# Beacon keys and first weights of a fused attention and MLP kernel: smaller loads, other queues, values split by even and odd d

## The chip, the cores and the metric

One core of a Trainium2 chip. The metric is the device time of one execution in microseconds (us), lower is better. All runs quoted are in the fast state unless said; the runs of one kernel spread over 0.1% to 1.4%. All kernels gave the reference's result.

## The reference

Attention over 8 batches of 8 heads, 576 queries and keys of width 64. Sixteen unmasked "beacon" keys and values stand ahead of the causal ones. The result, 4608 tokens of 512, goes through a two-layer MLP with a hidden width of 2048.

```python
k_all = np.concatenate([beacon_k, k], axis=2)          # 16 + 576 keys
v_all = np.concatenate([beacon_v, v], axis=2)
scores = scale * np.matmul(q, k_all.transpose(0, 1, 3, 2))
scores = np.where(causal, -1e9, scores)                # beacons are never masked
a = softmax(scores)
x = np.matmul(a, v_all)  ->  (B*S, H*D) = (4608, 512)
h = x @ w_in                                           # 512 x 2048
out = (h * sigmoid(1.702 * h)) @ w_out                 # 2048 x 512
```

## The kernel before

The heads are worked on in 16 sets of four, two sets to a batch; "set 2" is the first set of the second batch. The program first makes a list of operations with estimated durations and dependencies, runs a small scheduler over it, and issues every engine's instructions in the order that it found. Each engine then works through its own queue strictly in that order: **an instruction that waits holds up everything behind it on its engine**, whatever the scheduler had assumed of the wait. The traces show it: in the kernel before a cast waits 7.11 us on VectorE and the normalisation behind it starts at 26.98; with the cast moved (experiment 9) it starts at 19.86. That is what this case turns on.

The beacon keys of all sets stand in one tile, `bkf`, 32 partitions to a head. Loads of 32 rows fill the 32 partitions, though a head has 16 beacon rows; the other 16 are another head's. Sets 0 and 1 are loaded first; the rest is loaded in one batch after the first exponential:

```python
def e_load_bk(a, s0, s1):                      # head a of four, sets s0 to s1
    for u, e, nr in (...):                     # nr = 32 rows, 16 at the very end
        nc.sync.dma_start(
            out=bkf[32 * a : 32 * a + nr, u:e, :],
            in_=bass.AP(..., ap=[[D, nr], [Q * Nb * D, e - u], [1, D]]))
...
load_bk(0, HS)                                 # HS = 2: sets 0 and 1
...
            if (s, c) == (0, 0):
                later = op("DVE", 60, [exps[(0, 0)]], lambda: nc.vector.memset(bkf[:, HS, 0:1], 0.0), name="bk")
                load_bk(HS, NSET, [later])     # sets 2 to 15 at once
```

A set's keys begin with a cast of its beacon rows on VectorE; the transposes of keys and queries follow. "due" is a time before which the scheduler doesn't place an operation:

```python
cast = op(
    "DVE", 80, [ld_bk[s]] + turn.get((s - 2, 1), []), lambda: e_bk(s),
    pr=0 if urgent else 4, due=max(0, due_of(s, 0) - 10000), name=f"bk{s}",
)
```

The first weights, w1, are loaded by GpSimd in 16 transfers of 128 KB (as kept), four for each quarter of the columns. The rows are picked so that a chunk of 128 fits a half of each head's width: heads `a`, half `x`, row `r`:

```python
def e_load_w1(kt, c0, c1):
    hs, x = divmod(kt, 2)
    nc.gpsimd.dma_start(
        out=w1t[:, kt, c0:c1],
        in_=moe_w_in[:, c0:c1].rearrange("(g a x r) n -> g x a r n", g=HS, a=Q, x=2)[hs, x])
...
lhs = vb[b % NB2][0:kw, j, Q * hs + h, HD * x : HD * x + HD]     # values, half x of d
```

## Time and profile before

| before | value |
|---|---|
| time, median of 3 runs | 357.74 us (357.34 to 358.22) |
| span of the profiled execution | 355.7 us |
| TensorE busy, idle | 330.5 us, 25.2 us |
| beacon loads after the first exponential | three of 112 KB, one of 104 KB, one of 4 KB, on SP |
| their landing | 7.0 to 10.1 us after issue |
| w1 | 16 transfers, first issue at 7.8, last landing at 32.8 us |

Only TensorE is busy for most of the span (330.5 us; VectorE 202.1, ScalarE 201.3, GpSimd 113.2), so a microsecond of its idle time is a microsecond of the kernel. Some 20 of its 25 us of idle time lie in the first 27.5 us (13.1 and 7.3 in two stretches), so the start is what to read. The prediction below shows the lines.

The pages of DMA packets of the kernel before are needed later (queue, packets, MB, and the time that its packets took as a share of 16 engines' span; q0 is GpSimd's):

```profile
DMA packets 61223, 29.04 MB, mean 82 GB/s; under 512 B 48384, under 2 KB 52480, under 8 KB 61184
...
q0 software_dynamic: 53824, 18.51, 46.9%
```

### The profile page before, as it was taken

Reading aid. Unit: us, or ns where it says so; the run is one execution under the profiler, and the core shown is the slowest. Engines: PE = TensorE matmul, PEld = TensorE weight load, DVE = VectorE, ACT = ScalarE, POOL = GpSimd, SP = SyncE. Lnnn points to the kernel's source line nnn. Section 1 sums busy time; section 2 is a strip of 40 time slices with the busy share of each in tenths; the row PEclk is TensorE's granted clock in tenths of the full one; section 3 lists DMA queues with packets and bytes.
Section 4 is the critical chain, followed back from the end, with each engine's and each line's share of the span. In section 5 each row is a group of like instructions: output and inputs, shape, how many; then the busy total and the mean of one; then the engine's idle time right before and its main releaser. Section 6 shows DMA issues by size and latency. Waiting matters only on the chain.

```text
span 355.7 us, 9039 instructions
## 1 busy us (share of the span) xinstructions
PE 330.5 (93%) x3904; PEld 169.8 (48%) x3904; DVE 202.1 (57%) x385; ACT 201.3 (57%) x245; POOL 113.2 (32%) x192
## 2 busy tenths in 40 slices
PE   0529999999999999999999999999999999999995
PEld 0416665555545454545454545545445444444442
DVE  2816786768975759476665748485435444333300
ACT  1425577588856667776666576676553444444421
POOL 8746457257141913271264317230300000000000
PEclk9999999999999999999999999999999999999999
DMA  7999999259232942393439147800000110010011
GB/s 132 145 155 156 209 185 188 68 100 97 41 51 78 81 88 50 79 103 92 100 21 156 38 97 64 120 31 31 31 30 31 41 48 31 29 59 31 29 74 74
DMA packets 61223, 29.04 MB, mean 82 GB/s; under 512 B 48384, under 2 KB 52480, under 8 KB 61184
## 3 DMA queue, kind: packets, MB, share of 16 engines
q0 software_dynamic: 53824, 18.51, 46.9%
q1 hardware_dynamic: 7360, 9.96, 8.0%
q8 instruction: 30, 0.49, 0.6%
q14 instruction: 9, 0.07, 0.1%
HBM read 37.48 MB, written 9.44 MB: 132 GB/s over the span
## 4 chain that ended last, share of the span: by engine, by line
PE 82%; DMA 11%; POOL 3%; issue 1%; ACT 1%; DVE 1%; POOLq 0%; ACTq 0%
PE u L521 34%; PE u L488 32%; PE u L437 9%; PE s L374 7%; DMA w<-in_moe_w_in_dram 5%; DMA w<-in_moe_w_out_dram 4%; DMA qn<-in_q_dram 2%; POOL vb L308 1%; DVE g L509 1%; POOL kn L287 0%; POOL qn L287 0%; POOL E L413 0%; ACT sig L502 0%; ACT osb L535 0%; ACT E L385 0%
## 5 line engine op out<-in xcount | busy, mean ns | idle before, releaser
L509 DVE SCALAR_TENSOR_TENSOR g<-sig,u 128x512 f16<-128x512 f16 x144 | 97.6, 685 | 102.2 <-ACT sig L502 102.1
L488 PE MATMUL u<-xT,w 128*128 128x512 f16 (+1 forms) x640 | 147.5, 361 | 7.6 <-DVE xT L466 7.2
L521 PE MATMUL u<-w,g 128*128 128x512 f16 x576 | 143.8, 379 | 0.0
L502 ACT ACTIVATE sig<-u 128x512 f16<-128x512 f32 x144 | 85.2, 597 | 95.0 <-PE u L488 94.1
L385 ACT ACTIVATE E<-s 128x2048 f16<-128x2048 f32 (+2 forms) x64 | 99.6, 1556 | 35.4 <-PE s L374 34.8
L488 PEld LDWEIGHTS <-w 128*128 128x128 f16 x640 | 59.6, 98 | 69.0 <-DMA w<-in_moe_w_in_dram 7.5
L521 PEld LDWEIGHTS <-g 128*128 128x128 f16 x576 | 54.9, 98 | 65.0 <-issue 0.2
L413 POOL TENSOR_SCALAR_AFFINE_SELECT E<-E 128x448 f16<-128x448 f16 (+2 forms) x84 | 43.1, 538 | 123.5 <-ACT E L385 123.5
L374 PE MATMUL s<-qT,kT 32*128 32x288 f16 (+4 forms) x1152 | 37.0, 251 | 13.3 <-DVE kT L350 10.5
L374 PEld LDWEIGHTS <-kT 32*128 32x128 f16 x1152 | 22.8, 96 | 40.1 <-issue 25.9
L535 ACT ACTIVATE osb<-u 128x512 f32<-128x512 f32 x36 | 21.5, 598 | 20.0 <-PE u L521 19.9
L437 PE MATMUL u<-E,vb 128*32 128x288 f16 (+4 forms) x1024 | 29.9, 257 | 0.0
L308 POOL DMA_DIRECT2D vb<-in_v_dram x32 | 27.2, 871 | 2.7 <-DMA qn<-in_q_dram 1.6
L466 DVE TENSOR_TENSOR xT<-u,rz 128x288 f16<-128x288 f32 x64 | 26.5, 451 | 2.7 <-DVE rz L457 0.5
L437 PEld LDWEIGHTS <-vb 128*32 128x32 f16 (+1 forms) x1024 | 22.3, 98 | 2.8
L448 DVE STREAM_TRANSPOSE zt<-u 128x288 f32<-128x288 f32 x32 | 15.4, 480 | 11.5 <-PE u L437 11.5
L359 DVE STREAM_TRANSPOSE qT<-qn 128x576 f32<-128x576 f32 x16 | 19.9, 1241 | 1.6 <-PE s L374 1.6
L359 DVE STREAM_TRANSPOSE kT<-kn 128x576 f32<-128x576 f32 x16 | 20.1, 1257 | 0.6
L437 PE MATMUL u<-E,ones 128*32 128x288 f16 (+4 forms) x512 | 18.1, 260 | 0.4 <-ACT E L385 0.3
L457 DVE STREAM_TRANSPOSE rz<-rc 128x288 f32<-128x288 f32 x32 | 15.3, 478 | 1.1
L315 POOL DMA_DIRECT2D w<-in_moe_w_in_dram x16 | 10.8, 678 | 7.7 <-DMA w<-in_moe_w_in_dram 5.8
L437 PEld LDWEIGHTS <-ones 128*32 128x32 f16 (+1 forms) x512 | 11.0, 97 | 4.6 <-issue 2.1
(23 smaller groups left out, 52.8 us busy)
## 6 DMA issues: line engine op xcount, KB each, us to landing
out_dram<-osb SPq DMA_DIRECT2D x36, 256.0 KB, 2.0
kn<-in_k_dram POOLq DMA_DIRECT2D x16, 288.0 KB, 5.6
qn<-in_q_dram POOLq DMA_DIRECT2D x16, 288.0 KB, 5.5
vb<-in_v_dram POOLq DMA_DIRECT2D x24, 128.0 KB, 5.4
w<-in_moe_w_in_dram POOLq DMA_DIRECT2D x16, 128.0 KB, 8.4
w<-in_moe_w_out_dram POOLq DMA_DIRECT2D x4, 512.0 KB, 11.4
vb<-in_v_dram POOLq DMA_DIRECT2D x8, 112.0 KB, 3.6
vb<-in_v_dram POOLq DMA_DIRECT2D x8, 80.0 KB, 5.3
```

Source lines behind the costliest of these rows:

```text
L308: nc.gpsimd.dma_start(out=t[0 : hi - lo, j, h0:h1, :], in_=v[b, h0:h1, lo:hi, :].rearrange("h n d -> n h d"),)
L359: nc.vector.transpose(out=f32(dst.rearrange("p n e -> p (n e)")).rearrange("p (r t) -> p t r", t=n), in_=f32(src[:, o : o + n * D]).rearra ...
L374: nc.tensor.matmul(sc[:, h, o : o + e - a], kT[s % NB2][r : r + 32, j * P : (j + 1) * P, d], qT[s % NB2][r : r + 32, a:e, d], start=(d == ...
L385: nc.scalar.activation(out=Es[s][:, :, base[c] : base[c] + w], in_=ss[(s, c)][:, :, 0:w], func=AFT.Exp, scale=0.125,)
L413: nc.gpsimd.affine_select(out=blk, in_=blk, compare_op=ALU.is_ge, fill=0.0, base=off + (Nb if j == 0 else 0), pattern=[[0, Q], [1, w]], ch ...
L437: nc.tensor.matmul(u[32 * h : 32 * h + 32, a - q0 : e - q0], lhs, E[0:kw, h, col : col + e - a], start=(i == 0), stop=(i == n - 1),)
L466: nc.vector.tensor_tensor(out=xT[:, 2 * hs + x, t0 : t0 + HF], in0=rings[("av", s, x, half)][:, 0:HF], in1=zs[(s, half)][1][:, :], op=ALU. ...
L488: nc.tensor.matmul(u[:, o : o + w], w1t[:, kp, nt * P : (nt + 1) * P], xT[:, kp, t0:t1], start=(kp == 0), stop=(kp == NKT - 1),)
L502: nc.scalar.activation(out=sig[:, 0:w], in_=rings[("m1", g, n0)][:, 0:w], func=AFT.Tanh, scale=0.851)
L509: nc.vector.scalar_tensor_tensor(out=gts[g][:, n0:n1, 0:w], in0=sigs[(g, n0)][:, 0 : n * w].rearrange("p (n w) -> p n w", n=n), scalar=1.0 ...
L521: nc.tensor.matmul(o[:, :], gts[g][:, nt, mt * P : (mt + 1) * P], w2t[:, nt, :], start=(nt == 0), stop=(nt == NNT - 1),)
L535: nc.scalar.mul(out=osb[:, :], in_=rings[("m2", g, mt)][:, :], mul=0.5)
```

## The change

The intent: load only the beacon rows that are needed and clear the rest with a memset; put the loads of the very first set on two hardware queues (SP and ACT); load sets 2 and 3 right after the first exponential and the others later; give w1 as eight transfers of plain consecutive rows, which makes the values' halves the even and the odd columns of d; have at most eight of GpSimd's loads in flight in the scheduler's plan; and move the due times of the attention chunks a little. The plan's own reckoning of a beacon load changes with it: before, the data counted as there when the issue ends, now 2.5 us after that. Dead code (filler matmuls, split loads) goes too. Core of the diff:

```diff
-    nc.vector.memset(bkf[P - 32 : P, NSET - 1, :], 0.0)
+    nc.vector.memset(bkf[:, 0:1, :], 0.0)
+    nc.vector.memset(bkf[:, 1:HS, :], 0.0)
...
-    def e_load_w1(kt, c0, c1):
-        hs, x = divmod(kt, 2)
+    def e_load_w1(hs, c0, c1):
         nc.gpsimd.dma_start(
-            out=w1t[:, kt, c0:c1],
-            in_=moe_w_in[:, c0:c1].rearrange("(g a x r) n -> g x a r n", g=HS, a=Q, x=2)[hs, x],
+            out=w1t[:, 2 * hs : 2 * hs + 2, c0:c1],
+            in_=moe_w_in[2 * P * hs : 2 * P * (hs + 1), c0:c1].rearrange("(p x) n -> p x n", x=2),
         )
...
-    def e_load_bk(a, s0, s1):
-        (loads of 32 rows on nc.sync, see above)
+    def e_load_bk(a, s0, s1, e):
+        (nc.sync if e == "SP" else nc.scalar).dma_start(
+            out=bkf[32 * a : 32 * a + Nb, s0:s1, :],
+            in_=beacon_k.rearrange("b (g a) n d -> a n (b g) d", a=Q)[a][:, s0:s1, :],
+        )
...
-                    lhs = vb[b % NB2][0:kw, j, Q * hs + h, HD * x : HD * x + HD]
+                    lhs = vb[b % NB2][0:kw, j, Q * hs + h, x::2]
...
-    T_ATT0, T_ATT1 = 20000, 250000
+    T_ATT0, T_ATT1 = 15000, 255000
...
+    LANES = 8
+    flight = []
     def pool_load(dur, ns, deps, emit, due=0, pr=0, name=""):
+        if len(flight) >= LANES:
+            deps = list(deps) + [flight[-LANES]]
...
-    load_bk(0, HS)
+    load_bk(0, 1, (), ("SP", "ACT"))
+    load_bk(1, HS)
...
-                later = op("DVE", 60, [exps[(0, 0)]], lambda: nc.vector.memset(bkf[:, HS, 0:1], 0.0), name="bk")
-                load_bk(HS, NSET, [later])
+                for s0, s1, due in ((HS, 2 * HS, 12000), (2 * HS, NSET, 60000)):
+                    empty = op(
+                        "DVE", 60 * (s1 - s0), [exps[(0, 0)]],
+                        lambda s0=s0, s1=s1: nc.vector.memset(bkf[:, s0:s1, :], 0.0), due=due, pr=1, name="bk",
+                    )
+                    load_bk(s0, s1, [empty])
```

More of the change, by code (lines that the diff above doesn't have):

```diff
@@ L25, with __init__ @@
     LAT = {"PE": 230, "ACT": 100, "DVE": 135, "POOL": 60, "Q": 1400, "SP": 0}
-    def __init__(self, ring, filler=None, fill_from=1100, fill_to=15500):
-        self.filler, self.fill_from, self.fill_to = filler, fill_from, fill_to
+    def __init__(self, ring):
         self.ops = []
@@ L69, in run @@
         order = []
-        if self.filler:
-            o = self.op("-", 0, [], lambda: None)
-            self.ops.pop()
-            o.start, o.end = 0, self.fill_to
-            self.closers["fill"] = [o]
-            self.bank[-1] = "fill"
-            self.tiles["fill"] = len(self.bank) - 1
-            free["PE"] = self.fill_from
         todo = len(self.ops)
@@ L98, in run @@
             t, e = best
-            if self.filler and e == "PE" and free["PE"] < self.fill_to and t - free["PE"] > 400:
-                n = int((t - free["PE"] - 300) / 216)
-                if n > 0:
-                    o = self.op("PE", 0, [], lambda n=n: self.filler(n), kind="fill")
-                    self.ops.pop()
-                    o.start, o.end = free["PE"], t
-                    order.append(o)
-                    mode = "m"
             ok = []
@@ L135, in run @@
                 lat = self.LAT[o.eng] if u.eng != o.eng or o.eng in ("Q", "DVE", "POOL", "ACT") else 0
-                lat = 1200 if u.eng == "Q" else lat
+                if u.eng == "Q":
+                    lat = 300 if o.eng == "SP" else 1200
+                elif o.name == "bk" and o.eng != "DVE":
+                    lat = 2500
                 u.ready = max(u.ready, o.end + lat)
@@ L279, in ring_tile, with rows_of, e_load_qk @@
         return rings[key]
-    def e_load_qk(s, which, a, e):
+    def rows_of(t, s):
         b, hs = divmod(s, HS)
-        src, dst = ((q, qn), (k, kn))[which]
-        w = (e - a) // 32 * D
-        o = a // 32 * D
-        nc.gpsimd.dma_start(
-            out=dst[s % NB3][:, o : o + w],
-            in_=src[b, Q * hs : Q * hs + Q, a:e, :].rearrange("h (r t) d -> h r (t d)", r=32)
-            if e - a < S
-            else src[b, Q * hs : Q * hs + Q].rearrange("h (r t) d -> (h r) (t d)", r=32),
-        )
+        return t[b, Q * hs : Q * hs + Q].rearrange("h (r t) d -> (h r) (t d)", t=TR)
+    def e_load_qk(s, which):
+        dst = (qn, kn)[which][s % NB3]
+        nc.gpsimd.dma_start(out=dst[:, :], in_=rows_of((q, k)[which], s))
     def e_load_v(b, j, h0, h1):
@@ L325, in e_load_w2 @@
         )
-    def e_load_bk(a, s0, s1):
-        for u, e, nr in ((s0, min(s1, NSET - 1), 32), (max(s0, NSET - 1), s1, Nb)) if a == Q - 1 else (
-            (s0, s1, 32),
-        ):
-            if u < e:
-                nc.sync.dma_start(
-                    out=bkf[32 * a : 32 * a + nr, u:e, :],
-                    in_=bass.AP(
-                        tensor=beacon_k.tensor,
-                        offset=beacon_k.offset + (Q * u + a) * Nb * D,
-                        ap=[[D, nr], [Q * Nb * D, e - u], [1, D]],
-                    ),
-                )
+    def e_load_bk(a, s0, s1, e):
[3 more added lines that the diff above has]
+        )
     def e_bk(s):
@@ L345, in f32, with e_turn @@
         return ap.bitcast(F32)
-    def e_turn(s, which, a, e):
-        if which == 1 and a == 0:
+    def e_turn(s, which):
+        if which == 1:
             nc.vector.transpose(
@@ L353, in e_turn @@
             )
-        dst, src = (qT[s % NB2][:, a:e, :], qn[s % NB3])
+        dst, src = (qT[s % NB2][:, :, :], qn[s % NB3])
         if which == 1:
-            dst, src = (kT[s % NB2][:, Nb + a : Nb + e, :], kn[s % NB3])
-        n = (e - a) // 32
-        o = a // 32 * D
+            dst, src = (kT[s % NB2][:, Nb:NK, :], kn[s % NB3])
         nc.vector.transpose(
-            out=f32(dst.rearrange("p n e -> p (n e)")).rearrange("p (r t) -> p t r", t=n),
-            in_=f32(src[:, o : o + n * D]).rearrange("p (t c) -> p t c", t=n),
+            out=f32(dst.rearrange("p n e -> p (n e)")).rearrange("p (r t) -> p t r", t=TR),
+            in_=f32(src[:, :]).rearrange("p (t c) -> p t c", t=TR),
         )
@@ L548, in due_of @@
         return 0 if s < HS else T_ATT0 + T_CH * (4 * (s - HS) + c)
+    LANES = 8
+    flight = []
     def pool_load(dur, ns, deps, emit, due=0, pr=0, name=""):
+        if len(flight) >= LANES:
+            deps = list(deps) + [flight[-LANES]]
         i = plan.op("POOL", dur, deps, emit, due=due, pr=pr, name=name)
-        return plan.op("Q", ns, [i], lambda: None, name=name + "q")
+        flight.append(plan.op("Q", ns, [i], lambda: None, name=name + "q"))
+        return flight[-1]
     op = plan.op
@@ L559, with load_bk, load_qk @@
     chunks = []
-    SPLIT = 0
-    def parts(s):
-        return [(0, HF), (HF, S)] if s < SPLIT else [(0, S)]
-    def load_bk(s0, s1, deps=()):
-        got = [op("SP", 450, list(deps), lambda a=a: e_load_bk(a, s0, s1), name="bk") for a in range(Q)]
-        for s in range(s0, s1):
-            ld_bk[s] = got[-1]
-    def load_qk(s, which, i, due=0):
-        a, e = parts(s)[i]
-        dep = turn.get((s - NB3, which), [])
-        ld_qk[(s, which, i)] = pool_load(
-            560, 2.7 * (e - a) + (150 if e - a < S else 0), dep, lambda: e_load_qk(s, which, a, e),
-            due=due, name=f"ldqk{s}",
-        )
+    def load_bk(s0, s1, deps=(), queues=("SP",)):
+        got = []
+        for a in range(Q):
+            e = queues[a % len(queues)]
+            got.append(op(e, 450, list(deps), lambda a=a, e=e: e_load_bk(a, s0, s1, e), pr=0, name="bk"))
+        for s in range(s0, s1):
+            ld_bk[s] = got
+    def load_qk(s, which, due=0):
+        dep = [turn.get((s - NB3, which))]
+        ld_qk[(s, which)] = pool_load(560, 1560, dep, lambda: e_load_qk(s, which), due=due, name=f"ldqk{s}")
     def load_v(b, j, due=0):
@@ L588, in load_batch @@
             for which in (1, 0):
-                load_qk(s, which, 0, max(0, due_of(s, 0) - 22000))
+                load_qk(s, which, max(0, due_of(s, 0) - 22000))
         for j in range(-1, NJ):
@@ L594, in load_w1, with turns @@
         return [
-            pool_load(650, 5 * (c1 - c0) // 4 + 120, [], lambda kt=kt: e_load_w1(kt, c0, c1), due=due, name="w1")
-            for kt in range(NKT)
-        ]
-    def turn_part(s, i):
-        a, e = parts(s)[i]
+            pool_load(700, 5 * (c1 - c0) // 2, [], lambda hs=hs: e_load_w1(hs, c0, c1), due=due, name="w1")
+            for hs in range(HS)
+        ]
+    def turns(s):
         urgent = s < HS
-        if i == 0:
-            cast = op(
-                "DVE", 80, [ld_bk[s]] + turn.get((s - 2, 1), []), lambda: e_bk(s),
-                pr=0 if urgent else 4, due=max(0, due_of(s, 0) - 10000), name=f"bk{s}",
-            )
-        for which in (1, 0):
-            deps = [ld_qk[(s, which, i)]]
-            if i == 0:
-                deps += [qks.get((s - NB2, c)) for c in range(4)]
-                deps += [cast] if which else []
-            else:
-                deps += [qks[(s, 0)]]
-            turn.setdefault((s, which), []).append(
-                op(
-                    "DVE", 1.9 * (e - a) + (140 if which and not i else 0), deps,
-                    lambda which=which: e_turn(s, which, a, e),
-                    pr=i if urgent else 4, due=max(0, due_of(s, 0) - 9000), name=f"turn{s}",
-                )
+        cast = op(
+            "DVE", 80, ld_bk[s] + [turn.get((s - 2, 1))], lambda: e_bk(s),
+            pr=0 if urgent else 4, due=max(0, due_of(s, 0) - 10000), name=f"bk{s}",
+        )
+        for which in (1, 0):
+            deps = [ld_qk[(s, which)], cast if which else None]
+            turn[(s, which)] = op(
+                "DVE", 1095 + 140 * which, deps + [qks.get((s - NB2, c)) for c in range(4)],
+                lambda which=which: e_turn(s, which),
+                pr=0 if urgent else 4, due=max(0, due_of(s, 0) - 9000), name=f"turn{s}",
             )
@@ L623, in chunk @@
         if c == 0:
-            turn_part(s, 0)
-        deps = turn[(s, 0)] + turn[(s, 1)] + [exps[chunks[-1]] if chunks else None]
+            turns(s)
+        deps = [turn[(s, 0)], turn[(s, 1)]] + [exps[chunks[-1]] if chunks else None]
         chunks.append((s, c))
@@ L634, in chunk @@
         qks[(s, c)] = pe
-        if c == 0 and len(parts(s)) > 1:
-            turn_part(s, 1)
         exps[(s, c)] = op(
@@ L685, in w2_rows @@
         w2_ld.append(pool_load(750, 2600, [], lambda: e_load_w2(c), name="w2"))
-    load_bk(0, HS)
-    for s in range(HS):
-        load_qk(s, 1, 0)
-        load_qk(s, 0, 0)
-    keeps = op("POOL", 1200, [], e_keep, pr=0, name="keep")
+    load_bk(0, 1, (), ("SP", "ACT"))
+    load_bk(1, HS)
+    load_qk(0, 1)
+    load_qk(0, 0)
+    load_qk(1, 1)
+    load_qk(1, 0)
+    keeps = op("POOL", 1100, [], e_keep, pr=0, name="keep")
     for j in range(-1, 3):
         load_v(0, j)
-    for s in range(HS):
-        for i in range(1, len(parts(s))):
-            load_qk(s, 1, i)
-            load_qk(s, 0, i)
     w1_cols(0, 512)
@@ L706 @@
     for s in range(HS, 2 * HS):
-        load_qk(s, 1, 0)
-        load_qk(s, 0, 0)
+        load_qk(s, 1)
+        load_qk(s, 0)
     w2_rows(2)
@@ L758 @@
             if (s, c) == (0, 0):
-                later = op("DVE", 60, [exps[(0, 0)]], lambda: nc.vector.memset(bkf[:, HS, 0:1], 0.0), name="bk")
-                load_bk(HS, NSET, [later])
+                for s0, s1, due in ((HS, 2 * HS, 12000), (2 * HS, NSET, 60000)):
+                    empty = op(
+                        "DVE", 60 * (s1 - s0), [exps[(0, 0)]],
+                        lambda s0=s0, s1=s1: nc.vector.memset(bkf[:, s0:s1, :], 0.0), due=due, pr=1, name="bk",
+                    )
+                    load_bk(s0, s1, [empty])
         for s in range(HS * b, HS * b + HS):
```

## The prediction

> **What bounds the kernel now.** I read the summary and the 40 slices first, then the list of waits, then the timeline of the first 42 us, engine by engine, then the time to landing of each early load.
>
> The summary and the slices, one slice being 8.9 us:
>
> ```profile
> PE 330.5 (93%) x3904; PEld 169.8 (48%) x3904; DVE 202.1 (57%) x385; ACT 201.3 (57%) x245; POOL 113.2 (32%) x192
> ...
> PE   0529999999999999999999999999999999999995
> ...
> PEclk9999999999999999999999999999999999999999
> DMA  7999999259232942393439147800000110010011
> ```
>
> TensorE is the bound from the fourth slice to the last; its clock is full. Of a span of 355.7 us it is idle 25.2, and nearly all of that is in the first three slices. A table of stretches says how much: TensorE is busy 7.11 of the first 20.24 us, 0.00 of the next 7.25, 14.08 of the 14.39 after that, 17.88 of 18.12, 39.62 of 40, then 200.00 of 200. The tail holds another 4.14 us idle. So whatever brings the steady part forward moves the end by as much, and nothing else in this change does. The DMA row is the second thing to see: its 16 engines are at nine tenths for the first six slices.
>
> What stands in the gap, from the timelines of VectorE and of TensorE (start, duration, instruction, and in brackets the idle time before it and its releaser):
>
> ```profile
> 19.28 0.48 DVE L457 STREAM_TRANSPOSE rz<-rc 128x288 f32<-128x288 f32 x1
> 26.87 0.20 DVE L342 CAST bkn<-bkf 128x64 f16<-128x64 f32 x1 [7.11 <-DMA bkf<-in_beacon_k_dram]
> 26.98 0.82 DVE L466 TENSOR_TENSOR xT<-u,rz 128x288 f16<-128x288 f32 x2
> ```
>
> ```profile
> 10.49 1.04 PE L374 MATMUL s<-qT,kT 32*128 32x288 f16 x24 [10.49 <-DVE kT L350]
> 13.50 1.04 PE L374 MATMUL s<-qT,kT 32*128 32x288 f16 x24 [1.98 <-ACT E L385]
> ...
> 19.63 0.61 PE L488 MATMUL u<-xT,w 128*128 128x256 f16 x2
> 27.49 1.59 PE L488 MATMUL u<-xT,w 128*128 128x256 f16 x6 [7.25 <-DVE xT L466]
> ```
>
> A cast of the beacon keys of sets 2 to 15 stands in VectorE's queue ahead of the two normalisations that the MLP needs. The cast waits 7.11 us for its load; TensorE behind it waits 7.25. Before that, the first scores wait until 10.49, because the cast of sets 0 and 1 starts only at 7.36 (idle 6.12 on the beacon load).
>
> The list of waits also names a weight load at the same place:
>
> ```profile
> PEld L488 <- DMA w<-in_moe_w_in_dram: 7.5, 1, 7.5
> PE u L488 <- DVE xT L466: 7.2, 1, 7.2
> ```
>
> It isn't the cause. Issue plus landing gives 7.8 + 8.1 = 15.9 for the first w1 piece and 10.8 + 6.4 = 17.2 for the fourth, well ahead of 19.6; the normalisation ended last.
>
> [...] The five late beacon loads are 4 x 32 x 14 = 1792 rows of 256 B, 112 per engine; they land 7.0 to 10.1 us after issue, and the four w1 pieces beside them (columns 512 to 1023) need from 19.6 to 26.9 us, 7.3 us, where w2's 512 KB loads, four times such a piece, follow one another in 2.6. [...] here a v load (256 B rows in HBM, 128 KB kept) takes some 1.2 us, a 288 KB q or k load (4608 B rows) some 1.4. [...]
>
> **The change, part by part.**
>
> *Beacon bytes.* Before, each load takes 32 rows to fill 32 partitions, the upper 16 being another head's. After, 16 rows and a memset. The early loads go from 4 x 64 to 8 x 16 packets; the loads issued after the first exponential go from 1792 to 4 x 16 x 2 = 128; another 768 follow at about 50 us. That is 104 packets per engine fewer in the stretch from 15 to 27 us. Priced by the trace: w1 pieces need 2.6/4 = 0.65 us when alone, four are 2.6, so beacon cost 7.3 - 2.6 = 4.7 there, plus about 0.5 in the pieces on either side: 5.2 us, 50 ns a packet and engine. At the start another 8 packets an engine, 0.4 to 0.6. So **all later loads land about 5.7 us earlier**.
>
> *First scores.* The memset costs 0.1, then SP and ACT issue two loads each (0.38 to 0.43 each on SP), landing near 4 us by the 1.6 us of the first one before. kn lands at 1.30 + 4.3 = 5.6 and qn at 1.96 + 5.0 = 7.0, a little sooner now; transposes take 1.26 and 1.23. First scores near 8.2 instead of 10.49. The second pair is bound by its own loads (3.00 + 7.5 = 10.5 less 0.4, plus 1.25): 11.4 against 13.50. From there exp 1.88, scores, exp 1.40, mask, reciprocal, transpose run as before, 2 us earlier: VectorE is at the cast near 17.9.
>
> *The cast of set 2.* Its four loads are issued near 12.5, 8 packets an engine, and should have landed by 17. No wait. The normalisations follow and the MLP starts at about **18.5 instead of 27.49: 9.0 us gained so far**.
>
> *w1 in eight transfers.* Same rows of 2 KB, same bytes; 16 issues of 0.68 become 8 of some 0.7, on GpSimd, which waits for landings, not for issue. Worth nothing by itself. Its price, values read with a stride of two as weights, is nil by this trace: kT is already read so, 96 ns a weight load against 98 for packed vb.
>
> *Eight loads in flight, new due times.* They only reorder instructions; the order listings show 163 changes of matmul kind (scores, values, MLP) against 161, equal counts otherwise.
>
> *What is given back.* TensorE moves 9.0 us, the loads only 5.7, so every wait that had under 3.3 us of slack comes up. By the pace of before, the second 512 columns are wanted at 31.1 - 9.0 = 22.1 and land near 22; w2's second piece is wanted at 33.7 and lands near 32.5; both pass, just. The q and k of set 3 don't: before, the last landed at 32.0 + 12.3 = 44.3, so now near 38.6, and after's VectorE has both transposes of set 3 ahead of the four gates of the second token group. The first gate ends at 38.6 + 1.3 + 0.7 = 40.6. By then two PSUM banks hold unfinished output rows and two hold ungated MLP tiles, so TensorE, at 39.2 by its own pace, waits 1.4, or 2.0 if the loads are a little later. Take 1.7. For the loads of sets 4 to 15, which stand on SP behind three stores, and for smaller bubbles, 0.8.
>
> Sum: 9.0 - 1.7 - 0.8 = 6.5 us. 357.7 - 6.5 = **351.2**; I say 351.0, since the first wait may be shorter.
>
> **Rivals.** *The loads set the pace throughout* (DMA row at 9 for six slices, w2 landing as late as 48.8): then the gain is the 5.7 us of removed packets or less, with more waits from 20 to 45 us: 352 to 353.5. *The start was all VectorE's queue*: slack before was real (set 3's operands landed at 44.3, transposed at 48.5), no wait comes up, and the gain is 9: 348.7. *A new wait takes the old one's place*: the cast of set 4 waits for the second beacon batch (48 packets an engine, 2.4 us plus contention), which itself waits for a memset and three stores. At 0.1 us a packet under contention, 112 in 11 us as before, it needs 5 to 7 us, with about as much TensorE work beside it; if it stalls VectorE by 3 us, 353 to 354. Slower than before would need more than 9 us of new waits; nothing in the trace offers that.
>
> **Range and chances.** The rivals span 348.7 to 354; 80% in **348.2 to 354.2**. Two per cent is 350.6, just inside the centre: faster by over 2% 0.41, within 2% 0.58, slower 0.01.
>
> **What would show it.** The 7.11 us wait of the cast gone; first scores near 8.2, MLP from about 18.5; w1 in 8 issues and all landed by about 28 instead of 33; values' weight loads still 98 ns; TensorE idle 18 to 19 us instead of 25, with a new wait of 1 to 2 us near 39 to 41 behind set 3's transposes, steady part unchanged. Wrong would be: a wait for w1 or w2 of over 2 us between 20 and 35, a cast that waits near 50 to 60, or a steady part with new idle time.

## The result, and the profile after

| | before | after |
|---|---|---|
| median, us | 357.56 (357.34 to 358.22, 4 runs) | 353.68 (353.14 to 355.06, 4 runs) |
| ratio | 1 | 0.9894, 95% interval 0.986 to 0.9929 |
| span of the profiled execution, us | 355.7 | 353.2 |
| TensorE idle in it, us | 25.2 | 22.1 (353.2 - 331.1) |

A ratio here and below is the mean time of one kernel's fast runs over that of the other's of the same rounds, so not quite the ratio of the medians. The gain is 3.9 us by the medians where 6.7 were predicted (357.7 to 351.0). The result is within 2% and inside the range. The profiled execution of the changed kernel happens to be the slowest of its four runs (355.06), so its trace shows somewhat more waiting than a usual run has; experiments 6 and 7 will show how much.

Line numbers differ between the kernels: in the changed one the cast is L316, the normalisation L438, the MLP's first layer L460, scores L346, the gate L481. From the page of the kernel after:

```profile
PE 331.1 (94%) x3904; PEld 169.6 (48%) x3904; DVE 202.6 (57%) x387; ACT 201.2 (57%) x245; POOL 107.3 (30%) x184
...
PE   0569899999999999999999999999999999999995
...
PEclk9989999999999999999999999999999999999999
...
DMA packets 54055, 28.75 MB, mean 81 GB/s; under 512 B 41216, under 2 KB 45312, under 8 KB 54016
...
q0 software_dynamic: 47552, 18.49, 45.6%
```

TensorE's third slice has gone from 2 to 6, the second from 5 to 5: the gap has shrunk but is not gone, and the start is hardly earlier. One slice of the granted clock is new at 8. GpSimd's queue has 6272 packets fewer with the same bytes. The timeline of VectorE after shows what stands in the gap now:

```profile
8.69 0.20 DVE L316 CAST bkn<-bkf 128x64 f16<-128x64 f32 x1 [1.72 <-DMA bkf<-in_beacon_k_dram]
8.79 1.25 DVE L331 STREAM_TRANSPOSE qT<-qn 128x576 f32<-128x576 f32 x1
...
18.90 0.48 DVE L429 STREAM_TRANSPOSE rz<-rc 128x288 f32<-128x288 f32 x1
22.19 0.20 DVE L316 CAST bkn<-bkf 128x64 f16<-128x64 f32 x1 [2.81 <-DMA bkf<-in_beacon_k_dram]
22.30 0.82 DVE L438 TENSOR_TENSOR xT<-u,rz 128x288 f16<-128x288 f32 x2
```

The cast that waited 7.11 us still waits, 2.81, and again two normalisations are behind it. There is also a new wait, 1.72 at 8.69, of the cast of set 1, with the first set's query transpose behind it. TensorE's timeline after follows from that:

```profile
10.10 1.04 PE L346 MATMUL s<-qT,kT 32*128 32x288 f16 x24 [10.10 <-DVE kT L324]
13.12 1.04 PE L346 MATMUL s<-qT,kT 32*128 32x288 f16 x24 [1.98 <-ACT E L357]
...
22.80 1.59 PE L460 MATMUL u<-xT,w 128*128 128x256 f16 x6 [3.03 <-DVE xT L438]
...
44.28 1.03 PE L460 MATMUL u<-xT,w 128*128 128x256 f16 x8 [0.94 <-DVE g L481]
```

First scores at 10.10 instead of 10.49 (predicted near 8.2); the MLP at 22.80 instead of 27.49 (predicted 18.5); a gate wait of 0.94 near 44 (predicted 1.4 to 2.0 near 39 to 41). Of the 9.0 us predicted for the MLP's start, 4.7 came.

How long the loads themselves took is in the view of one tile's instructions, here `bkf` in two windows of the kernel after. First the last two of set 1's four loads, then set 2's and 3's four (the first line of each gives how many, the time that issuing took in ns, and the first and last start):

```profile
L310 SPq DMA_DIRECT2D bkf<-in_beacon_k_dram x2: 420/420/420, 2.9 to 3.3; - x2
...
DMA to landing us min/median/max: 5.2/5.3/5.3
```

```profile
L310 SPq DMA_DIRECT2D bkf<-in_beacon_k_dram x4: 328/427/454, 14.2 to 15.6; - x4
...
DMA to landing us min/median/max: 4.8/5.1/6.5
```

Loads of 4 and 8 KB take about 5 us here, where the plan reckons 2.5 from the end of the issue. The first such loads, issued at 1.0 before GpSimd's first load (1.3), landed 1.5 to 1.7 later.

### The profile page after: what moved, and what is told of

Same layout as the page of the kernel before. It is cut to its first block, busy times and chain, and to the rows that moved or that the text cites. A ratio compares the mean times of both kernels' runs of the same rounds, so it can differ in the third digit from the quotient of the medians.

```text
span 353.2 us, 9037 instructions
## 1 busy us (share of the span) xinstructions
PE 331.1 (94%) x3904; PEld 169.6 (48%) x3904; DVE 202.6 (57%) x387; ACT 201.2 (57%) x245; POOL 107.3 (30%) x184
## 3 DMA queue, kind: packets, MB, share of 16 engines
q0 software_dynamic: 47552, 18.49, 45.6%
## 4 chain that ended last, share of the span: by engine, by line
PE 86%; DVE 4%; DMA 3%; ACT 3%; issue 2%; SPq 1%; DVEq 0%; ACTq 0%
PE u L493 35%; PE u L460 34%; PE u L409 9%; PE s L346 8%; DMA bkf<-in_beacon_k_dram 3%; ACT E L357 1%; ACT sig L474 1%; DVE g L481 1%; SPq L310 1%; DVE qT L331 1%; DVE xT L438 1%; DVE kT L331 0%; DVE E L378 0%; DVE zt L420 0%; ACT osb L507 0%
## 5 line engine op out<-in xcount | busy, mean ns | idle before, releaser
L481 DVE SCALAR_TENSOR_TENSOR g<-sig,u 128x512 f16<-128x512 f16 x144 | 97.4, 684 | 100.4 <-ACT sig L474 100.4
L460 PE MATMUL u<-xT,w 128*128 128x512 f16 (+1 forms) x640 | 147.5, 361 | 4.6 <-DVE xT L438 3.4
L460 PEld LDWEIGHTS <-w 128*128 128x128 f16 x640 | 59.9, 99 | 66.9 <-issue 9.1
L346 PE MATMUL s<-qT,kT 32*128 32x288 f16 (+4 forms) x1152 | 37.0, 251 | 13.1 <-DVE kT L324 10.1
L346 PEld LDWEIGHTS <-kT 32*128 32x128 f16 x1152 | 22.7, 96 | 39.2 <-issue 27.4
L507 ACT ACTIVATE osb<-u 128x512 f32<-128x512 f32 x36 | 21.5, 598 | 23.1 <-PE u L493 23.1
L291 POOL DMA_DIRECT2D vb<-in_v_dram x32 | 27.2, 864 | 3.4 <-DMA qn<-in_q_dram 2.2
L438 DVE TENSOR_TENSOR xT<-u,rz 128x288 f16<-128x288 f32 x64 | 26.4, 451 | 2.7 <-PE u L460 0.4
L409 PE MATMUL u<-E,ones 128*32 128x288 f16 (+4 forms) x512 | 17.9, 260 | 0.3 <-ACT E L357 0.3
L275 POOL DMA_DIRECT2D kn<-in_k_dram x16 | 9.1, 568 | 1.8 <-DMA w<-in_moe_w_in_dram 0.9
```

The lines of the kernel that those rows point to most:

```text
L291: nc.gpsimd.dma_start(out=t[0 : hi - lo, j, h0:h1, :], in_=v[b, h0:h1, lo:hi, :].rearrange("h n d -> n h d"),)
L346: nc.tensor.matmul(sc[:, h, o : o + e - a], kT[s % NB2][r : r + 32, j * P : (j + 1) * P, d], qT[s % NB2][r : r + 32, a:e, d], start=(d == ...
L409: nc.tensor.matmul(u[32 * h : 32 * h + 32, a - q0 : e - q0], lhs, E[0:kw, h, col : col + e - a], start=(i == 0), stop=(i == n - 1),)
L438: nc.vector.tensor_tensor(out=xT[:, 2 * hs + x, t0 : t0 + HF], in0=rings[("av", s, x, half)][:, 0:HF], in1=zs[(s, half)][1][:, :], op=ALU. ...
L460: nc.tensor.matmul(u[:, o : o + w], w1t[:, kp, nt * P : (nt + 1) * P], xT[:, kp, t0:t1], start=(kp == 0), stop=(kp == NKT - 1),)
L481: nc.vector.scalar_tensor_tensor(out=gts[g][:, n0:n1, 0:w], in0=sigs[(g, n0)][:, 0 : n * w].rearrange("p (n w) -> p n w", n=n), scalar=1.0 ...
```

## The experiments

The theory after the result, **theory A**: what was mis-sized is the landing of the small beacon loads. Beside a busy GpSimd queue they take about 5 us whatever their size; both casts wait for that in VectorE's queue, and that is where the missing microseconds went. Rivals: the loads' packets still compete and the missing gain is w1 (B); the due times or the limit of eight loads cost what the rest gains (C); the missing gain is the granted clock, new at 8 in one slice (D). The experiments ran in three sessions of four on three chips, each against the kernel before in the same session, five rounds each.

**1. Sets 2 and 3 loaded at the start.** Edit to the changed kernel; the loads have three times the rows and are issued 12 us earlier.

```diff
-    nc.vector.memset(bkf[:, 1:HS, :], 0.0)
+    nc.vector.memset(bkf[:, 1 : 2 * HS, :], 0.0)
-    load_bk(1, HS)
+    load_bk(1, 2 * HS)
-    for s0, s1, due in ((HS, 2 * HS, 12000), (2 * HS, NSET, 60000)):
+    for s0, s1, due in ((2 * HS, NSET, 60000),):
```

(The cast of set 2 is also kept behind set 1's transposes, so that it can't move ahead of them.)

> The changed kernel with the beacon loads of sets 2 and 3 issued at the start together with set 1's, and set 2's cast after set 1's transposes. Theory A (the changed kernel lost most of the missing gain to a small beacon load that waits some 5 us in a busy transfer queue whatever its size, so that set 2's cast still holds up VectorE for 2.8 us): the wait before the normalisations goes, the MLP starts at about 20 instead of 22.8, and the time falls by 2 to 3 us against the changed kernel, ratio to before about 0.982. Rival B (the loads of w1, q and k pace TensorE anyway): the MLP starts earlier but new waits of the same size follow before 45 us, the time stays within 0.7 us of the changed kernel's, ratio about 0.989.

Ratio 0.9822 (0.9791 to 0.9853), median 351.52 against 357.68. The wait of set 2's cast is gone and the MLP starts at 19.50. First scores stay late, 10.36, with set 1's cast waiting 2.03. The landing view of the four loads, with 16 x 3 rows of 256 B each in place of 16:

```profile
L310 SPq DMA_DIRECT2D bkf<-in_beacon_k_dram x4: 413/424/425, 1.9 to 3.3; - x4
...
DMA to landing us min/median/max: 3.8/5.1/5.5
```

**Three times the packets land no later** (3.8 to 5.5, where the changed kernel's four take 3.8 to 5.3). Between 16 and 48 rows, the number of a load's own packets is not what sets its landing. Where the prediction priced 50 to 100 ns a packet and engine, the price of loads this small is some 4 to 6.5 us each. Larger ones do take longer: the three loads of 448 rows (112 KB) in the kernel before landed after 7.0 to 8.1 us.

**2. The cast of set 1 behind set 0's transposes.** Edit to the changed kernel:

```diff
-    "DVE", 80, ld_bk[s] + [turn.get((s - 2, 1))], lambda: e_bk(s),
+    "DVE", 80, ld_bk[s] + [turn.get((s - 2, 1)), turn.get((0, 0)) if s == 1 else None], lambda: e_bk(s),
```

> The changed kernel with the cast of set 1's beacon keys moved behind the transposition of set 0's q. Theory A: first scores at about 8.3 instead of 10.1; the second pair is then bound by its own q load at about 11.9 instead of 13.1; but set 2's cast still waits for loads issued only some 1.2 us earlier, so the MLP starts at about 21.6 and the time falls by about 1 us, ratio to before about 0.986. Rival B: no change, 0.989.

Ratio 0.9855 (0.9821 to 0.989), median 353.01. First scores 8.40, the second pair 11.42, so the predicted 8.2 and 11.4 were right but for the order of one cast. Set 2's cast, reached at 17.6, still waits 1.77 and the MLP starts at 19.96 (expected 21.6). By the medians the edit is worth only 0.7 us, not the 2.8 us by which the MLP starts earlier than in the trace of the changed kernel. That trace is one with a long wait; in experiments 6 and 7 the MLP starts near 20.7, less than 1 us later than here.

**3. Both.** The edits of 1 and 2 together.

> Both edits together. Theory A: first scores at about 8.3, no wait for beacon loads after that, the MLP starts at about 18.6 as the prediction had it; then the waits for later loads that the prediction named come up and take back 1 to 2 us, so the time is 349.5 to 351, ratio to before 0.977 to 0.982. Rival B: 0.987 to 0.989.

Ratio 0.9801 (0.9765 to 0.9838), median 350.81: 6.9 us under before, and at 351.0 the time that was predicted for the change itself. The timelines of VectorE and of TensorE in this run:

```profile
9.29 0.19 DVE L316 CAST bkn<-bkf 128x64 f16<-128x64 f32 x1 [0.98 <-DMA bkf<-in_beacon_k_dram]
```

```profile
8.36 1.04 PE L346 MATMUL s<-qT,kT 32*128 32x288 f16 x24 [8.36 <-DVE qT L331]
...
18.29 2.33 PE L460 MATMUL u<-xT,w 128*128 128x256 f16 x8
...
25.22 1.05 PE L460 MATMUL u<-xT,w 128*128 128x256 f16 x8
...
39.92 1.03 PE L460 MATMUL u<-xT,w 128*128 128x256 f16 x8 [0.93 <-DVE g L481]
```

First scores 8.36 (predicted 8.2), MLP 18.29 (18.5). With the two waits out of the way of the first scores and of the MLP, both start within 0.2 us of the predicted times, and the total agrees too. The second pair of scores comes at 12.15 where 11.4 was predicted, as set 1's cast still waits 0.98 ahead of it. Experiments 1 to 3 together show theory A: each wait that is moved away brings the start forward, and both together the time, clear of the intervals (0.9765 to 0.9838 against 0.986 to 0.9929).

**4. w1 alone.** The kernel before, with only the eight plain w1 transfers and the strided values.

> The kernel before with only w1 in eight plain transfers and the values read with a stride of two. The prediction: worth nothing by itself, ratio 0.998 to 1.002, w1 landings as before within 1 us. Rival C (the old w1 transfers carry many tiny packets, which the trace of before shows as thousands of 4-byte packets between 12 and 30 us, and the four-byte packets slow the queue): all of w1 lands 3 to 5 us earlier, the late beacon loads land some 2 us earlier, and the time falls by about 2 us, ratio about 0.994.

Ratio **1.0165** (1.0134 to 1.0197), median 363.97: 6.3 us slower than before. VectorE and TensorE:

```profile
31.30 0.20 DVE L341 CAST bkn<-bkf 128x64 f16<-128x64 f32 x1 [11.54 <-DMA bkf<-in_beacon_k_dram]
```

```profile
31.91 1.59 PE L487 MATMUL u<-xT,w 128*128 128x256 f16 x6 [11.67 <-DVE xT L465]
```

Neither expectation had this sign. w1's last transfer is now issued at 16.2 and landed at 27.2, in place of 27.2 and 32.8; the late beacon loads, the same ones as before, land 8.2 to 15.2 us after issue in place of 7.0 to 10.1, and the cast's wait grows from 7.11 to 11.54. These 4.4 us are most of the 6.3 lost; of the rest, an estimated 1.2 is half pace (16 matmuls take 3.59 us at 34.16, and 1.92 in experiment 8), which here lasts until 37.7, 5.8 us of MLP work, where before it ended at 30.9 after 3.4. So the form of w1 is not neutral: its loads are issued on GpSimd within 8.4 us (7.8 to 16.2) in place of 19.4, and the loads on SP land later.

**5. Beacon alone.** The changed kernel with the 16 old w1 transfers and packed values.

> The changed kernel with w1 back in sixteen transfers and the values in packed order: the beacon part and the new plan alone. The prediction's step (beacon rows are what slowed the w1 pieces beside them, 4.7 us): the second 512 columns of w1 land near 22, as in the changed kernel, and the time is within 0.7 us of the changed kernel's, ratio about 0.989. Rival C (the old w1 transfers are slow by themselves): the late beacon loads land sooner than in the changed kernel because the queue beside them is slower, so set 2's cast waits under 2.8 us, but w1 lands as late as 26 us or more for its second 512 columns and TensorE waits for it from about 23, w1 is complete only near 30; ratio about 0.989 to 0.993 with the idle time in another place.

Ratio 1.0049 (1.0011 to 1.0088), median 359.4 of seven fast runs against 358.0 (an eighth, slow, took 363.9): no gain at all. TensorE's timeline names two waits; VectorE's follows:

```profile
22.42 1.31 PE L461 MATMUL u<-xT,w 128*128 128x256 f16 x6 [2.72 <-DMA w<-in_moe_w_in_dram]
...
73.70 0.64 PE L347 MATMUL s<-qT,kT 32*128 32x288 f16 x24 [2.80 <-DVE kT L325]
74.27 4.02 PE L461 MATMUL u<-xT,w 128*128 128x512 f16 x10
```

```profile
21.81 0.20 DVE L317 CAST bkn<-bkf 128x64 f16<-128x64 f32 x1 [2.59 <-DMA bkf<-in_beacon_k_dram]
21.91 0.82 DVE L439 TENSOR_TENSOR xT<-u,rz 128x288 f16<-128x288 f32 x2
```

The MLP starts at 22.42, much as in the changed kernel. The profile names w1 as its releaser, but the matmul waits for two semaphores, that of a w1 piece landed at 15.7 (a later transfer uses it again near 22) and that of the normalisation. The first normalisation ended at 22.37; in the changed kernel too the MLP starts 0.05 us after it. So it is set 2's cast again, with 2.59, that holds TensorE up, as the prediction read it in the kernel before. w1 in its old form is landed only by 30.0 (last issue at 23.4, 6.6 to land), and no wait for it follows. At 71.9 the cast of set 4 waits 2.30 for the second batch of beacon loads, behind stores on SP; this is the prediction's third rival, which in the changed kernel shows as only 0.71. Ten matmuls at 74.27 then take 4.02 us: the clock is granted at half from 74.3 to 77.7, and twelve such matmuls at 79.09 take 2.76. The wait of 2.80 and, as an estimate, half of these 3.4 us make 4.5 of the 5.7 us by which this kernel's median lies above the changed one's.

Experiments 4 and 5 are the two parts of the change. Neither gains (1.0165 and 1.0049), together they give 0.9894: **each part alone runs into a wait that eats its gain**. For w1 alone it is the cast, which the beacon part shortens. For the beacon part alone it is the second batch, which is a matter of when that batch is issued (experiment 11).

**6. The old due times**, and **7. no limit on loads in flight.** Edits to the changed kernel:

```diff
-    T_ATT0, T_ATT1 = 15000, 255000
+    T_ATT0, T_ATT1 = 20000, 250000
```

```diff
-    LANES = 8
+    LANES = 1000
```

> The changed kernel with the old due times (20000 and 250000). The prediction: only a reordering, ratio within 0.002 of the changed kernel's 0.989. Rival: the later end of the attention is worth something in the steady part; then it is 1 us or more slower, 0.992 or above.

> The changed kernel with the plan's limit of eight loads in flight lifted (1000), so that the plan puts the loads of the third batch ahead of set 2's masks on GpSimd, as the kernel before did. The prediction: no change, ratio 0.987 to 0.991. Rival: GpSimd sits waiting for a free load while the masks of set 2 are due, TensorE waits for the masks between 45 and 60 us, and the time is 1 to 2 us longer, 0.992 to 0.995.

Ratios 0.9883 (0.9843 to 0.9923) and 0.9884 (0.9857 to 0.991), medians 353.47 and 353.67, against 0.9894 of the change: neither matters in this kernel, and theory C falls. Their traces say something else: set 2's cast waits only 1.05 and 0.81 us, and the MLP starts at 20.86 and 20.61 rather than 22.80, at equal median times. So the landing of one 8 KB load varies by about 2 us between these traces (the cast behind it starts at 20.24 and 20.00 there, at 22.19 here), and the trace of the changed kernel that was kept is one with a long wait. Its semaphore's record shows where: of the last load's sixteen increments fifteen had come by 20.25 and one came at 22.07. An instruction fetch of 16 KB stood in the DMA queues from 19.80 to 20.74, just ahead of the late packet at 20.80; that it was the cause isn't shown.

**8. Both, with the start's loads on two queues.** Edit to experiment 3:

```diff
-    load_bk(1, 2 * HS)
+    load_bk(1, 2 * HS, (), ("SP", "ACT"))
```

> The kernel of e3 (beacon loads of sets 1 to 3 at the start, casts behind the transposes) with those loads split over SP and ACT, so that the last is issued near 2.4 instead of 3.3. If a small load's time to landing grows with the moment of its issue (3.8 us at 2.4, 5.4 at 3.3), set 1's cast no longer waits 0.98 us, the second pair of scores moves from 12.15 to about 11.4, and the time falls by up to 0.7 us against e3, ratio to before 0.978 to 0.980. If not, it equals e3.

Ratio 0.9782 (0.9753 to 0.9811), median 350.09. Set 1's cast no longer waits (it starts at 8.10, with no idle time before it), and TensorE reaches its full pace some 4 us earlier: its MLP matmuls run at full pace from 17.6 on (two take 0.39 us at 17.55, six 1.07 at 18.63), where in experiment 3 they do so from 21.3 (eight take 2.33 us at 18.29, and 16 take 1.96 from 21.29). By the times the difference from experiment 3 is within the intervals and stays unproven.

**9. The kernel before with only the order mended.** One edit to the kernel before: the cast of set 2 comes later in VectorE's queue, nothing else.

```diff
-    pr=0 if urgent else 4, due=max(0, due_of(s, 0) - 10000), name=f"bk{s}",
+    pr=0 if urgent else 4, due=30000 if s == HS else max(0, due_of(s, 0) - 10000), name=f"bk{s}",
```

> The kernel before with one edit: set 2's cast has a due time of 30 us in the plan, which puts it behind the normalisations that it held up; every load is as before. Theory A (what the change gained came from that wait alone): the MLP starts at about 20.3 instead of 27.5; the second 512 columns of w1 land at 26.9 as before and are wanted at 24, so some 3 us come back as a wait for w1; ratio 0.988 to 0.991, as much as the whole change. Rival: the beacon packets still pace w1, q and k and all 7 us come back; ratio 0.998 to 1.002.

Ratio **1.0052** (1.0034 to 1.007), median 359.8 of 22 runs: slower, where theory A as it then stood asked for 0.988 to 0.991. It falls in this form. TensorE and GpSimd in this run:

```profile
20.37 1.07 PE L488 MATMUL u<-xT,w 128*128 128x256 f16 x6 [0.69 <-DVE xT L466]
...
26.84 0.72 PE L488 MATMUL u<-xT,w 128*128 128x256 f16 x5 [3.65 <-DMA w<-in_moe_w_in_dram]
...
56.98 0.23 PE L437 MATMUL u<-E,ones 128*32 128x48 f16 x4 [4.08 <-POOL E L413]
```

```profile
53.15 3.39 POOL L308 DMA_DIRECT2D vb<-in_v_dram  x4
56.51 1.25 POOL L413 TENSOR_SCALAR_AFFINE_SELECT E<-E 128x192 f16<-128x192 f16 x3
```

The MLP does start 7.1 us earlier, at 20.37. But w1 isn't there: 3.65 us of wait at 26.84. Then, near 57, a mask that TensorE needs stands on GpSimd behind the issue of four value loads, 4.08 us, and the granted clock is at half from 55.8 to 62.6. What was gained at the start is lost by then, and a little more.

**10. w1 and the order.** Experiment 4 with the edit of experiment 9.

> The kernel of e4 (w1 in eight plain transfers, which made the kernel before 1.65% slower) with the same due time for set 2's cast. Theory A (e4 was slower only because the denser loads on GpSimd's queue let the beacon loads land at 31.3 instead of 26.9 and the cast waited for them): the loss turns into a gain; w1 lands well ahead of its use, the MLP starts at about 20.3, and the ratio is 0.981 to 0.986, better than e9 by 1.5 to 3 us, which is what w1's form is worth once the wait is off the path. Rival: the strided values or the plain form cost time in the steady part; then it stays above 0.99.

Ratio 0.9821 (0.9783 to 0.9859), median 352.03. The same edit of one due time that made the kernel before 0.5% slower turns w1's +1.65% into -1.8%. With the cast out of the way, the form of w1 is worth 1.0052 - 0.9821, 2.3% or about 8 us. The beacon loads here are the old, large ones: **the packets that the change removes don't have to go for this gain; the wait at the head of VectorE's queue does**. The cast still waits, but later, and TensorE only for a gate behind it:

```profile
31.62 0.20 DVE L341 CAST bkn<-bkf 128x64 f16<-128x64 f32 x1 [3.27 <-DMA bkf<-in_beacon_k_dram]
```

```profile
20.60 1.07 PE L487 MATMUL u<-xT,w 128*128 128x256 f16 x6 [0.68 <-DVE xT L465]
33.03 0.68 PE L436 MATMUL u<-E,ones 128*32 128x288 f16 x20 [1.41 <-DVE g L508]
```

What in w1's form does it isn't separated: GpSimd's issuing also falls, from 16 transfers (10.8 us) to 8 (5.6).

**11. Beacon alone, second batch earlier.** Experiment 5 with:

```diff
-    (2 * HS, NSET, 60000)
+    (2 * HS, NSET, 30000)
```

> The kernel of e5 (beacon part alone, 1.005) with the second beacon batch (sets 4 to 15) due at 30 us in the plan instead of 60, ahead of the stores on SP. Theory A (e5 kept the gain of the start, but set 4's cast then waited 2.3 us near 70 us for the batch behind three stores, and TensorE 2.8 us for its transposes): that wait goes, ratio 0.990 to 0.995. Rival (w1's old form costs the difference): stays at 1.000 to 1.006.

Ratio 0.9908 (0.9874 to 0.9941), median 355.2, within the 0.990 to 0.995 expected. The wait near 72 is gone and with it 1.4%, so experiment 5's loss was mostly this one. The MLP still starts at 22.74, behind set 2's cast (2.64 us). With the old w1 the beacon part so gains nearly as much as the whole change (0.9894), and the rival, that w1's old form costs the difference, falls. The changed kernel itself was not run with this edit alone.

**12. All of it.** Experiment 8 with the second batch at 30000.

> The fastest so far, e8 (0.9782), with the second beacon batch due at 30 us in the plan. Theory A: the cast of set 4 had waited little there, so 0 to 1 us less, ratio 0.976 to 0.978. Rival: 768 more beacon packets among the loads of w2, q and k between 30 and 45 us delay those, 0.979 to 0.982.

Ratio **0.975** (0.9713 to 0.9788), median 349.64 (349.49 to 350.0): 8.4 us under before and some 4 (by the medians of two sessions) to 5 (by the ratios) under the changed kernel, the fastest of the study and the only one that is faster than before by over 2% with its whole interval. Its TensorE is idle 18.6 us (347.6 - 329.0):

```profile
17.77 0.39 PE L460 MATMUL u<-xT,w 128*128 128x256 f16 x2
18.85 1.07 PE L460 MATMUL u<-xT,w 128*128 128x256 f16 x6 [0.69 <-DVE xT L438]
```

Against experiment 8 it gains 0.3%, within both intervals, so that the earlier batch helps here is not shown.

**The clock, theory D.** The slice at 8 is in this table of stretches of the kernel after (busy microseconds of each engine with instruction counts, then the granted clock, DMA share, GB/s):

```profile
22.90:26.40 3.50, 3.40 (x29) 1.79 (x28) 1.47 (x4) 1.83 (x2) 2.03 (x3) 0.51 1.24 205
26.40:30.00 3.60, 3.60 (x91) 2.87 (x90) 2.38 (x6) 2.65 (x4) 0.55 (x1) 1.00 1.23 211
```

A gap of 3.03 us is followed by 3.41 us at half clock (23.0 to 26.4), worth an estimated half of that, 1.7 us. Gaps of 2.45 us in experiment 2 (mean granted clock 0.51 from 21.7 to 25.2) and of 1.50 in experiment 7 (0.995 over its span of 351.3, so some 3.5 us at half) were followed by about as long a stretch at half, while after the 3.65 us in experiment 9 the matmuls keep full pace (five in 0.72 us at 26.84, eight in 1.05 at 29.53); what decides isn't shown. But this is no loss against before: in the profile before, the six MLP matmuls at 27.49 take 1.59 us as they do here at 22.80, and the pace of its first-layer matmuls (from one start to the next) is half until 30.8. The granted clock reads 1.00 there all the same; the first record of that row is at 30.87 in the profile before (at 19.56 in the one after), so it says nothing of the pace ahead of it. In experiment 12 the same six matmuls take 1.07. So D accounts for an estimated 1.5 us between experiment 3 (2.33 us for eight matmuls at 18.29, 1.05 for eight later) and experiment 12, and nothing between before and after.

## Why the prediction was right or wrong

- **What bounds the kernel** was right: with TensorE's start brought forward the end follows. The gain in TensorE's lost time is made by 30 us and mostly kept. As an estimate, time minus the least time that the matmuls issued so far need at the traces' full pace (its level depends on the pace taken for the small shapes, the differences between kernels hardly): before 25.6, after 21.7, experiment 3 17.9 us at 30 us; 45.6, 42.9 and 38.6 at 300 us.
- **The cast as the cause** of the gap was right, though it is set 2's alone, not that of sets 2 to 15. "It isn't the cause" of the w1 wait was right too: experiment 9 keeps the old w1 and the old beacon loads and moves the cast, and the MLP starts at 20.37.
- **"Should have landed by 17. No wait" failed**, and is the largest term. The loads took 4.8 to 6.5 us, where eight packets an engine at the prediction's price make 0.4 to 0.8, and its own times leave some 3 for the last. They were issued at 14.2 to 15.6 rather than near 12.5, but only because the first scores were late: in experiment 2, with these at 8.40, the issue is at 12.5 to 13.9 as predicted, each load takes 5.0 to 5.3, and the cast waits 1.77 all the same. The trace of before had such a landing in it: the fourth early load, issued at 2.17, took 5.1. In the trace kept that is 2.8 us at the MLP's start; in the usual run perhaps 1 (experiments 6 and 7).
- **"First scores near 8.2" failed for the same reason**: set 1's cast, whose last loads took 5.3 us, stood ahead of set 0's query transpose. They came at 10.10; VectorE reached set 2's cast at 19.4 rather than 17.9. The two terms, 1.5 and 2.8, are the 4.3 us by which the MLP missed 18.5. Experiments 2 and 3 give 8.40 and 8.36 once the order is mended.
- **"w1 ... worth nothing by itself" was wrong in both directions.** By itself it costs 6.3 us (experiment 4), and with the cast moved it is worth about 8 (9 against 10). Only beside the beacon part with its second batch early is it worth next to nothing: 0.9908 without it (experiment 11), 0.9894 with it. The bytes are the same and so are the rows; the prediction looked at those and not at the packets. The old transfers bring 6272 more packets of 4 B to GpSimd's queue, 392 a transfer. By the trace's own record of each packet, those of 4 B took 5.5 us an engine before and 1.5 after, and the 1 KB packets of the weights, w2 included, 28.4 and 25.5 (4096 at 111 and at 99 ns, over 16 engines): 6.9 us together, and w1 is landed by 25.3, 7.5 us earlier than before.
- **"beacon cost 5.2 us" was near as a size, but not the whole cause.** The prediction laid the slow w1 pieces from 19.6 to 26.9 at the beacon loads' door, 4.7 us (its estimate: 7.3 less the 2.6 of four such pieces alone). With those nearly gone but the old w1 form (experiment 5) these pieces are landed by 23.1, 3.9 us earlier; with the new form and all the old beacon loads (experiment 4) by 20.2, with both by 20.4, so either edit does it. All of w1 is landed by 30.0, 27.2 and 25.3, after 32.8 before: the form of w1 has the larger part. So "all later loads 5.7 us earlier" was short: set 3's last load landed 7.7 us earlier (36.6 after 44.3).
- **"What is given back"** was near in sum. By the lost time above, of 4.7 us gained at the MLP's start 3.9 are left at 30 us and 2.7 at 300 us: 2.0 given back where 2.5 were predicted, with the gate wait, 0.94 for 1.7, the largest named piece. It stands where it was foretold, behind set 3's transposes, but not for the reason given: these don't wait for a load, whose last had landed at 36.6. VectorE works from 38.0 to 43.7 without a pause, mostly on the transposes of sets 2 and 3. In experiment 3 the 9.2 us at the start are 7.7 and 7.0: 2.2 given back.
- **Values with a stride of two cost nothing**: 98 ns a weight load, as predicted. The due times and the limit on loads did nothing, as predicted.
- **The rivals.** The third, a cast waiting for the second batch, is there in small (0.71) and in full in experiment 5 (2.30, with half clock after it). The first, loads setting the pace, gave nearly the right size, 352 to 353.5 against 353.68, but by luck: the loads that set it are the small ones, not the removed packets.
- **"its clock is full"** missed the half pace after 27.5 (six matmuls in 1.59 us, in 1.07 in experiment 12), which the row of the granted clock doesn't show. It costs before and after the same, so no number of the prediction changed.

So direction, place and chain were right and the size was off: 9.0 us at the MLP's start was 4.7, of which 2 were given back in the trace kept. What stays open is why a small load on a hardware queue takes 5 us beside GpSimd's queue, and why that varies by 2 us. The trace's record of each packet narrows it. In the kernel after, the first packet of set 2's and 3's loads is recorded at 17.98, 3.8 us after the first issue, and the last landing comes 0.5 us after their last packet; at the kernel's start the first packet is recorded 1.0 us after the issue. So most of the 5 us pass before the first packet of a small load is recorded. For the large loads of the kernel before, the last landing comes 2.1 us after their last packet (24.93 and 26.99). No run took GpSimd's loads away, so what holds the packets back isn't shown. Why the old w1 rearrangement brings the extra 4 B packets isn't shown either, only that they come and go with it.

## What to carry to other kernels

On an engine with a strict queue, price a small load by the landing of another small load under the same traffic, not by its bytes or packets (some 4 to 6.5 us here with 16 to 48 rows), and place the instruction that waits for it behind everything that doesn't need it; with w1's new form, moving one cast did here what removing 1700 packets was meant to do, while without it the same move lost 0.5%. If a plan sets the order, give it the measured landing. Count the packets of a rearranged transfer in the profile, since equal bytes and rows can hide several microseconds of DMA time (an estimated 6.9 an engine here). Where two parts change each other's waits, test them together and apart before judging either: here the halves read +1.65% and +0.5% and their sum -1.1%, and the second read -0.9% once one batch of loads was issued earlier. When a wait has several semaphores, check the named releaser against the times of landing.
